# A delta-net and gated feed-forward kernel: order of all work from a list scheduler, and two units inverted in one pass

## The chip, the cores and the metric

One core of one Trainium2 chip. The metric is the device time of one execution in microseconds (us), as the median of the runs of a job. The span is the part of an execution that the profile covers; it is some 2 us shorter than the time. The granted clock is the share of full speed that TensorE was allowed, as the profile records it (PEclk). The core's engines are TensorE (PE in the profile, PEld its weight loads), VectorE (DVE), ScalarE (ACT), GpSimd (POOL) and SyncE (SP, which here only issues transfers).

## The reference

Two blocks follow each other. The first is a delta rule over 768 steps, for 4 batches of 8 heads of width 48:

```python
k_n = k / (np.linalg.norm(k, axis=-1, keepdims=True) + 1e-06)
for t in range(S):
    y[:, :, t] = np.einsum('bhd,bhde->bhe', q[:, :, t], state)
    v_old = np.einsum('bhde,bhd->bhe', state, kt)
    state = state + bt[:, :, :, None] * np.einsum('bhd,bhe->bhde', kt, vt - v_old)
```

The second takes y as 3072 tokens of 384 features through two layers, 384 to 2048 to 384, all in fp32 (the weights arrive in fp64):

```python
h = x @ w_in
g = h * np.cos(h)
return g @ w_out
```

## The kernel before

The 768 steps are cut into 24 units of 32 steps. A unit needs: transposes of k and q (`turn`, p_t), Gram products (`gram`, p_g), the inverse z of a unit lower triangular 32x32 matrix for each head and batch (`invert`), a product with the state (p_kq), a solve with z (p_u), an update of the state (p_s), an inner product (p_kq again), and transposes into the feature layout (p_z, copied into x_ffn). Two units make a pair of 256 tokens, and a pair needs 8 groups of products of the first layer (p_h) and 8 of the second (p_o).

The matrix to invert goes out to DRAM (g_dr), comes back with one head of one batch on each partition (gb), is inverted by elimination there, and goes out and back once more (z_dr, zt):

```python
def invert(n, tag=None):                 # before: one unit, 4 partitions for a matrix (SPLIT = 4)
    ...
    for j in range(C - 1):               # C = 32
        rows = j // SPLIT + 1
        shape = [128, rows, C - 1 - j]
        ...
        eng.tensor_tensor(out=part, in0=z[:, 0:rows, j, None].to_broadcast(shape),
                          in1=a[:, j, None, j + 1 :].to_broadcast(shape), op=ALU.mult)
        behind = z[:, 0:rows, j + 1 :]
        eng.tensor_tensor(out=behind, in0=behind, in1=part, op=ALU.subtract)
```

`eng` is GpSimd, for units 0 and 2 DVE. Weights come as pairs of 32-bit words and are narrowed to fp32 by two ACT steps, two DVE steps and one GpSimd addition for each of 28 tiles.

Which piece of work comes when is written out by hand, some 130 lines of calls for the head and a loop for the rest; at the end every instruction is tied to the one before it on its engine, so no engine may take another order:

```python
    inverting = {0: invert(0, "one"), 1: invert(1), 2: invert(2, "o")}
    invert_next(0, 1)
    invert_next(1, 6)
    narrow_load(2)
    ...
    for s in range(4, NU + 4):
        load(s + 8, "k")
        ...
        through_state(s)
        invert_next(s + 1, 2)
        gated(1)
        ...
```

## Time and profile before

| | before |
| --- | --- |
| time, median of 3 runs | 780.71 us (780.11 to 782.49) |
| span of the profiled run | 777.6 us |
| PE busy | 682.3 us, 88% of the span |
| DVE, ACT, POOL busy | 46%, 37%, 64% |
| bytes moved by DMA | 55.41 MB |

The share of 88% is an average over two very different stretches: it is 100% from about 200 us on, and far less before.

### The profile page before, as it was taken

How to read it: one execution, taken by the hardware profiler on the slowest of the kernel's cores; microseconds unless marked ns; L12 is line 12 of the kernel's file. 1: busy time of each engine (PE TensorE's matmuls, PEld its weight loads, DVE VectorE, ACT ScalarE, POOL GpSimd, SP SyncE). 2: the span in 40 equal slices, each digit the busy share in tenths (PEclk: the TensorE clock that was granted, in tenths of full speed). 3: DMA queues.
4: the chain of work that ended last, by engine and by line, in shares of the span. 5: the costliest groups of instructions: out<-in, count | busy, mean ns of one | idle time of the engine just before them, and what ended most of it. 6: DMA issues, size and time to landing. Idle time of an engine off the chain costs nothing.

```text
span 777.6 us, 24710 instructions
## 1 busy us (share of the span) xinstructions
PE 682.3 (88%) x10472; PEld 504.7 (65%) x10472; DVE 360.1 (46%) x694; ACT 286.8 (37%) x506; POOL 499.7 (64%) x1423
## 2 busy tenths in 40 slices
PE   4134786655999999999999999999999999999996
PEld 3133564433777777777777777777777777777763
DVE  4675765445345444444444444454444444433430
ACT  3021643344244334334434334443443333333330
POOL 6753877838877868768868678688668667710000
PEclk9995887778899999999999999999999999999999
DMA  7844567362223422332342233123222210010000
GB/s 128 221 105 111 118 133 196 82 178 69 55 49 78 88 46 58 82 62 49 72 91 44 56 83 65 45 66 77 47 47 57 61 24 10 19 25 11 10 12 20
DMA packets 164559, 55.41 MB, mean 71 GB/s; under 512 B 154512, under 2 KB 157584, under 8 KB 164448
## 3 DMA queue, kind: packets, MB, share of 16 engines
q1 hardware_dynamic: 161872, 52.79, 31.3%
q8 instruction: 82, 1.34, 0.7%
q0 software_dynamic: 448, 0.71, 0.4%
q10 hardware_dynamic: 2128, 0.33, 0.2%
q14 instruction: 29, 0.24, 0.1%
HBM read 42.78 MB, written 11.01 MB: 69 GB/s over the span
## 4 chain that ended last, share of the span: by engine, by line
PE 75%; POOL 8%; DMA 2%; issue 2%; SPq 1%; ACT 1%; DVE 0%; POOLq 0%; ACTq 0%
PE p_o L580 33%; PE p_h L552 29%; PE p_kq L447 3%; POOL z L407 3%; POOL part L400 2%; PE p_kq L504 2%; PE p_u L470 2%; PE p_t L324 2%; PE p_s L492 2%; PE p_g L340 2%; POOL w_in L225 1%; POOL w_out L225 1%; DMA gb<-g_dr 1%; PE p_z L525 1%; POOL knrm L273 1%
## 5 line engine op out<-in xcount | busy, mean ns | idle before, releaser
L552 PE MATMUL p_h<-x_ffn,w_in 128*128 128x256 f32 x1152 | 277.4, 391 | 23.4 <-POOL w_in L225 10.5
L580 PE MATMUL p_o<-w_out,g_ffn 128*128 128x384 f32 x768 | 273.4, 499 | 15.7 <-POOL w_out L225 15.0
L552 PEld LDWEIGHTS p_h<-x_ffn,w_in 128*128 128x128 f32 x1152 | 224.9, 197 | 78.4 <-POOL w_in L225 13.1
L400 POOL TENSOR_TENSOR part<-z,gb 128x60 f32<-128x60 f32 (+24 forms) x682 | 213.1, 312 | 90.4 <-ACT z L391 29.1
L407 POOL TENSOR_TENSOR z<-z,part 128x60 f32<-128x60 f32 (+24 forms) x682 | 212.1, 311 | 53.4
L580 PEld LDWEIGHTS p_o<-w_out,g_ffn 128*128 128x128 f32 x768 | 139.7, 191 | 101.8 <-POOL w_out L225 20.2
L564 DVE SCALAR_TENSOR_TENSOR r<-turns,p_h 128x512 f32<-128x512 int32 x96 | 65.9, 687 | 267.5 <-ACT turns L562 267.5
L562 ACT ACTIVATE turns<-p_h 128x512 int32<-128x512 f32 x96 | 57.2, 596 | 264.9 <-PE p_h L552 264.9
L544 DVE TENSOR_TENSOR g_ffn<-r,p_h 128x512 f32<-128x512 f32 x96 | 66.0, 687 | 66.0 <-ACT r L539 58.8
L538 ACT ACTIVATE r<-r 128x512 f32<-128x512 f32 x96 | 60.6, 631 | 72.3 <-DVE r L567 72.3
L539 ACT ACTIVATE r<-r,halfpi 128x512 f32<-128x512 f32 x96 | 69.3, 722 | 3.1
L567 DVE SCALAR_TENSOR_TENSOR r<-turns,r 128x512 f32<-128x512 int32 x96 | 68.2, 710 | 3.3
L273 POOL TENSOR_TENSOR knrm<-ksum,halves 128x16 f32<-128x16 f32 (+1 forms) x14 | 35.9, 2567 | 11.5 <-DVE ksum L270 10.5
L447 PEld LDWEIGHTS p_kq<-st,kq_t 48*32 48x32 f32 x2944 | 29.5, 106 | 7.6 <-issue 7.5
L326 ACT COPY kq_t<-p_t 128x512 f32<-128x512 f32 x48 | 25.8, 591 | 23.0 <-PE p_t L324 23.0
L447 PE MATMUL p_kq<-st,kq_t 48*32 48x48 f32 x2944 | 32.7, 213 | 0.0
L219 DVE SCALAR_TENSOR_TENSOR pairs<-pairs 128x384 uint32<-128x384 uint32 (+1 forms) x28 | 19.2, 686 | 24.4 <-ACT pairs L218 23.5
L470 PE MATMUL p_u<-rhs,zt 32*32 32x48 f32 x1472 | 23.0, 211 | 8.0 <-DMA zt<-z_dr 5.8
L340 PE MATMUL p_g<-kq_t 48*32 48x64 f32 x1536 | 22.4, 245 | 6.4 <-ACT kq_t L326 4.7
L513 ACT COPY y<-p_kq 128x384 f32<-128x384 f32 x24 | 11.5, 478 | 44.4 <-PE p_kq L504 44.4
L340 PEld LDWEIGHTS p_g<-kq_t 48*32 48x32 f32 x1536 | 18.2, 116 | 14.5 <-issue 6.3
L324 PE MATMUL p_t<-consts,qp 128*128 128x128 f32 x96 | 17.7, 316 | 10.8 <-DMA qp<-in_q_dram 10.8
(56 smaller groups left out, 449.2 us busy)
## 6 DMA issues: line engine op xcount, KB each, us to landing
gb<-g_dr SPq DMA_DIRECT2D x96, 128.0 KB
pairs<-in_moe_w_in_dram SPq DMA_DIRECT2D x12, 512.0 KB
pairs<-in_moe_w_out_dram SPq DMA_DIRECT2D x16, 384.0 KB
vp<-in_v_dram SPq DMA_DIRECT2D x96, 48.0 KB
out_dram<-o SPq DMA_DIRECT2D x24, 192.0 KB
qp<-in_q_dram SPq DMA_DIRECT2D x92, 48.0 KB
kp<-in_k_dram SPq DMA_DIRECT2D x88, 48.0 KB
z_dr<-z SPq DMA_DIRECT2D x24, 128.0 KB
```

Of the source, the lines that this page charges most:

```text
L340: nc.tensor.matmul(p_g[quarter(b), par, j], kq_t[rows48(par), 0, j, quarter(b)], kq_t[rows48(par), :, j, quarter(b)],)
L400: eng.tensor_tensor(out=part, in0=z[:, 0:rows, j, None].to_broadcast(shape), in1=a[:, j, None, j + 1 :].to_broadcast(shape), op=ALU.mult,)
L407: eng.tensor_tensor(out=behind, in0=behind, in1=part, op=ALU.subtract)
L447: nc.tensor.matmul(p_kq[quarter(b), par, a, j], kq_t[rows48(par), a, j, quarter(b)], st[rows48(par), b // 2, j, b % 2], start=(j == 0 and ...
L538: nc.scalar.activation(r, r, AF.Abs)
L539: nc.scalar.activation(r, r, AF.Sin, bias=halfpi, scale=-1.0 / SCALE)
L544: nc.vector.tensor_tensor(out=gates[p][f // 4][:, f % 4 : f % 4 + 2], in0=r, in1=p_h, op=ALU.mult)
L552: nc.tensor.matmul(p_h[:, i], w_in[:, t, (f + i) * 128 : (f + i + 1) * 128], x[:, t], start=(t == 0), stop=(t == KT - 1),)
L562: nc.scalar.activation(turns, p_h, AF.Copy, scale=1.0 / (2.0 * math.pi * SCALE))
L564: nc.vector.scalar_tensor_tensor(out=r, in0=turns, scalar=-PI2_HI * SCALE, in1=p_h, op0=ALU.mult, op1=ALU.add)
L567: nc.vector.scalar_tensor_tensor(out=r, in0=turns, scalar=-PI2_LO * SCALE, in1=r, op0=ALU.mult, op1=ALU.add)
L580: nc.tensor.matmul(p_o, gs[f // 4][:, f % 4, i * 128 : (i + 1) * 128], w_out[:, f], start=(f == 0), stop=(f == FT - 1),)
```

## The change

Its intent is to replace the hand-written order by one that a program finds when the kernel is built. Each piece of work becomes a task with an engine, a cost in us, the tasks it depends on, the buffers it takes and frees, and a time by which it is due. A list scheduler then walks through time, and each engine that is free takes the ready task that is due first. The instructions are written in that order and tied to it as before. The second part inverts the two units of a pair in one pass: 64 matrices on 128 partitions, two partitions for each, in place of four.

```diff
-SPLIT = 4
+SPLIT = 2
...
+class Order:
+    WINDOW = 132.4
+    LAG = {"PE": 0.2, "DVE": 0.15, "ACT": 0.15, "POOL": 0.2, "SP": 2.0}
+    IN_FLIGHT = 8
...
+    def run(self, wrote):
...
+            for engine, heap in ready.items():
+                if free[engine] > now:
+                    continue
+                put_back, item = [], None
+                while heap and heap[0][0] <= limit:      # earliest due first
+                    item = heapq.heappop(heap)
...
+                    if fits(item[2]):                    # are its buffers free?
+                        break
...
+                emit()                                   # the instructions are written now
...
+                free[engine] = start + cost
...
-    def invert(n, tag=None):
+    def invert(m, tag, columns):                         # m: a pair of units
...
+    VECTOR = {0: "one"}                                  # only the first pair on DVE
+    W_IN, W_OUT, LOADS = 0.3, 101.9, -30.5               # due times of the weights
+    START = 55.7
+    FIRST, STEP = 5, 5.73
...
+        ends = [0, 4, 8, 12, 16, 20, 24, C - 1]
+        for i, (x, y) in enumerate(zip(ends, ends[1:])):
+            each = (0.2, 0.001) if held else (0.245, 0.00175)     # DVE, GpSimd: us per instruction, per element
+            cost = sum(2 * (each[0] + each[1] * (j // SPLIT + 1) * (C - 1 - j)) for j in range(x, y))
+            add(("inv", m, i), "DVE" if held else "POOL", cost, ...)
...
+            add(("hidden", *key), "PE", 2.62, lambda f=f: hidden(p, f), deps, ...)
+            add(("gate", *key), "DVE", 0.73, lambda f=f: hidden_gate(p, f), ...)
...
-    norms(0, one)
-    load(3, "k", nc.gpsimd)
-    load(2, "k")
-    turn(0)
-    ...                                                  # 200 lines of order by hand
+    log = order.run(wrote)
```

## The prediction

> **What bounds the kernel now.** I read the 40 slices of the page first, then the busy times by stretch, then the chain that ended last, then the waits of the first 200 us.
>
> The slices (19.4 us each; the digits are tenths of busy time):
>
> ```profile
> PE   4134786655999999999999999999999999999996
> POOL 6753877838877868768868678688668667710000
> PEclk9995887778899999999999999999999999999999
> DMA  7844567362223422332342233123222210010000
> ```
>
> There are two regimes. From slice 11 (about 200 us) to the end TensorE is busy at full clock. Before that it is neither busy nor at full clock, and no other engine is full either. The stretches give the sizes (length, then busy us of each engine, granted clock, DMA share):
>
> ```profile
> core 0: us, PE busy (x) PEld busy (x) DVE busy (x) ACT busy (x) POOL busy (x), PEclk, DMA share, GB/s
> 0.00:76.76 76.76, 28.14 (x751) 22.52 (x751) 48.42 (x183) 16.19 (x33) 45.30 (x111) 0.88 0.64 139
> 76.76:200.94 124.18, 84.30 (x1337) 60.61 (x1337) 64.63 (x118) 55.58 (x104) 90.26 (x190) 0.78 0.52 125
> 200.94:771.40 570.46, 569.83 (x8386) 421.54 (x8385) 247.07 (x393) 214.51 (x370) 364.15 (x1123) 1.00 0.25 51
> 255.05:309.20 54.15, 54.15 (x896) 40.59 (x901) 24.94 (x41) 21.31 (x37) 41.30 (x126) 1.00 0.32 66
> ```
>
> The cuts are mine: 76.76 is the start of the first p_h product, 771.40 the last p_o product, and 255.05 to 309.20 one pair of units in the steady part. A pair costs TensorE 54.15 us at full clock. The chain of waits shows 2.59 us for a p_h group and 2.58 us for four p_o blocks; a pair has 8 of each, 41.3 us, so two units of delta-net work take 12.85 us. Twelve pairs are 649.8 us; unit 0 has no product with the state (1.42) and unit 23 no update (about 0.8): **TensorE owes about 648 us at full clock**. Since 570 of these lie after 200.94, only 78 us' worth was done in the first 201 us. **The loss is 201 - 78 = 123 us**, and after 771.4 come 6.2 us of last copy and store. That loss is the only thing of size to win.
>
> The loss is not one bound but hand-over after hand-over. The waits of the first 200 us:
>
> ```profile
> ACT w_out L216 <- DMA pairs<-in_moe_w_out_dram: 26.9, 4, 11.6
> DVE pairs L219 <- ACT pairs L218: 23.5, 9, 10.9
> PE p_u L470 <- DMA zt<-z_dr: 19.8, 8, 13.1
> POOL w_out L225 <- DVE w_out L224: 16.4, 3, 8.0
> PE p_o L580 <- POOL w_out L225: 15.0, 4, 7.0
> PE p_t L324 <- DMA qp<-in_q_dram: 10.8, 1, 10.8
> PE p_h L552 <- POOL w_in L225: 10.5, 5, 6.4
> ```
>
> ACT stands before a weight load that has not landed, DVE behind ACT, GpSimd behind DVE, TensorE behind GpSimd. And the chain that ended last shows why the weight was late:
>
> ```profile
> 145.24 2.26 DMA z_dr<-z
> 154.12 4.54 DMA gb<-g_dr
> 162.41 3.27 DMA pairs<-in_moe_w_out_dram
> 178.20 3.90 POOL w_out L225 x4
> 193.57 4.21 PE p_o L580 x6
> ```
>
> In between (not shown) lie the SyncE issues of zt, of the q, k, v loads and of gb: the weight load was queued behind a put that waited for an inversion. The order written by hand costs the time, not the amount of work.
>
> **What the Trainium skill says.** "TensorE: Matmul & The Clock Gate", section "Architectural detail: the array is 16× 32×32, not 1× 128×128", says that ACT, DVE and GpSimd run their instructions strictly in order. The trace agrees: the 26.9 us above are a whole engine held by one load. The same page, Part 1, says that the clock falls to half after an idle window and comes back after some 3.4 us of work. It agrees: from 60 to 80 us the granted clock is 0.50, and the first p_h group takes 5.46 us instead of 2.59. So filling gaps pays twice. "GPSIMD Engine Reference", section 3.1, says that an element costs GpSimd more than DVE and that dispatch is a large fixed part; here the 60-element product takes 0.30 us on GpSimd (undisturbed) and 0.22 on DVE. "DMA: Bandwidth & Descriptors", section Specifications, puts line rate at 512 B or more; of 164559 packets 154512 are under 512 B, and the first 40 us have a DMA share of 0.81 at only 176 GB/s. DMA is the scarce thing there.
>
> **The change, part by part.**
>
> *Inversion.* Per unit: 31 steps of two instructions, 62 in all, 1560 elements per partition for each of the two kinds (sum of rows times columns left). Per pair with two rows' shares: still 62 instructions, 2856 elements for each kind. GpSimd goes from 0.21 us (8 elements) to 0.325 (76), so about 0.195 + 0.0017 per element, plus 0.075 between instructions. Unit now: 62 x 0.27 + 3120 x 0.0017 = 22.0 us (the trace: 23.0 to 45.9). Pair after: 62 x 0.27 + 5712 x 0.0017 = 26.4 us instead of 44. GpSimd falls from 41 to about 25 busy us per 54; as TensorE is full there, this by itself is worth nothing after 200 us. In the head it frees GpSimd for the 28 weight additions (32 us). On DVE (0.163 + 0.001 per element, 0.04 between): the first pair takes 62 x 0.203 + 5.7 = 18.3 us; before, units 0 and 2 were done there.
>
> *Traffic.* gb was fetched four times per unit, 96 x 128 KB = 12.6 MB. Now it is twice per pair, 24 x 256 KB = 6.3 MB. In the first 40 us that is 1 MB of some 7.
>
> *First p_h.* Before: unit 0 was solved at 51.1 us, but unit 1 only at 66.0, because its z was put and fetched through the SyncE queue separately; p_h began at 76.76. After: both come out of one inversion. g of unit 1 is ready at 15.5; put and fetch about 6 us with no queue ahead, more with the weight loads, which the due times put first: inversion starts at 22 to 26. With 18.3 us and about 3 us of other DVE work it ends at 44 to 47. From its end to the end of the first solve were 8.6 us (42.5 to 51.1). Then, from the trace's durations: u 1.0, p_s 1.5, st 1.0, p_kq 1.4, rhs 0.55, second solve 1.5, u 1.0, p_s and the inner product 3.0, y 0.5, p_z 0.6, x 0.5: 12.6 us. **First p_h at 65 to 68, say 66.**
>
> *After that.* Done by then: units 0 and 1 and the transposes and Gram products of some four more, about 18 us' worth, leaving 630. Weights are loaded as early as buffers allow, so the first and second layer of pair 0 and units 2 and 3 all offer work, and I allow 8 us for cold clock and gaps from 66 to about 120 (before: of the 78 us' worth some 16 were done by 76.76, so 62 fell into the 124 us up to 200.94, a loss of 62 us).
>
> *Steady part and tail.* The due-time rule reaches for the next ready task. Its costs (2.62 for a p_h group, 0.9, 0.85, 1.4 for the small ones) sum to 54.2 us per pair, which is what the trace shows, and its DVE and ACT costs are slightly above the trace's. I expect no large waits. The tail stays: 6 us.
>
> **Sum:** 66 + 630 + 8 + 6 = 710 us of span, and the time is some 2 to 3 us above the span (780.7 against 777.6): **712 us**.
>
> **The rivals.**
> 1. *Fine waits on TensorE.* Before, at least one p_o and one p_h group (5.2 us) lay between two small products of a unit, which hid DVE and ACT. The list may place them the moment its model calls them ready. If 6 hand-overs of each of 24 units cost 0.3 us, that is 43 us, and the time is about 755. For: orders are pinned, so an error of the model is a wait. Against: a 2.6 us block usually lies between, and the costs match.
> 2. *DMA holds the head.* Ten weight loads at the front are 5 MB, at 176 GB/s almost 30 us; the put and fetch of g queue behind them, the first p_h comes at 78 or so, with the weights ready. Then 78 + 630 + 6 + 6 + 2.5: about 723. For: share 0.81 already. Against: half of gb is gone, and large loads run above the mean rate.
> 3. *Shared buffers.* Weight pairs and gates share ten buffers; weights of the second layer waiting for narrowing could hold the gates, or ACT and DVE (28 x 1.3 and 28 x 1.1 us of narrowing) become the bound from 60 to 130. About 735. Against: between 76.76 and 200.94 DVE is 52% and ACT 45% busy.
> 4. *Only the inversion counts*, order is neutral: first p_h 10 us earlier, the rest as before, about 768. Against: the waits above are order.
>
> **Range and chances.** Rivals 2 and 3 in part are likely and set the upper end; the lower end is a first p_h at 60 with no loss after it. 698 to 733. Over 2% faster means under 765; only rival 4 or two rivals in full miss it: 0.94. Within 2%: 0.04; slower: 0.02.
>
> **What would show it.** Right: p_h first at about 66; TensorE near 90% busy from about 70 and full clock from 90; the steady pair still 54 us; GpSimd's inversion groups half the count, and about 430 busy us down to about 240; gb 24 issues; ACT's wait for w_out gone. Wrong: TensorE waits spread over the steady part (rival 1), zt waits beyond 70 us (rival 2), gates waiting for GpSimd (rival 3), or a second half where pairs take over 55 us.

## More of the kernel before

The cosine of the first layer is done like this, for each p_h group:

```python
nc.scalar.activation(turns, p_h, AF.Copy, scale=1.0 / (2.0 * math.pi * SCALE))   # ACT, to int32
nc.vector.scalar_tensor_tensor(out=r, in0=turns, scalar=-PI2_HI * SCALE, in1=p_h, ...)  # DVE, 1st reduction step
nc.vector.scalar_tensor_tensor(out=r, in0=turns, scalar=-PI2_LO * SCALE, in1=r, ...)    # DVE, 2nd reduction step
nc.scalar.activation(r, r, AF.Abs)
nc.scalar.activation(r, r, AF.Sin, bias=halfpi, scale=-1.0 / SCALE)
nc.vector.tensor_tensor(out=gates..., in0=r, in1=p_h, op=ALU.mult)               # DVE, the gate: frees p_h's bank
```

p_h lies in PSUM, in a buffer that the text calls a bank. The kernel has two of them, so the p_h group after the next can't start before the gate has freed one.

## The result and the profile after

Faster, by less than half of what I had predicted. Ratios in this document are the mean time of one kernel's fast runs over that of the other's fast runs of the same rounds, so they are not quite the ratios of the medians beside them.

| | before | after | predicted |
| --- | --- | --- | --- |
| time, median of 4 runs each | 781.04 us | 754.67 us (754.30 to 759.42) | 712 (698 to 733) |
| ratio | | 0.9675 (95% interval 0.9633 to 0.9716) | 0.91 |
| span of the profiled run | 777.6 us | 752.7 us | 710 |
| first p_h product | 76.8 us | 79.2 us | 66 |
| a pair of units in the steady part | 54.15 us | 54.2 to 57.9 us | 54 |
| POOL busy | 499.7 us | 345.6 us | |
| bytes moved by DMA | 55.41 MB | 49.18 MB | 49.1 |

The slices of the changed kernel (18.8 us each, tenths of busy time):

```profile
PE   3206899798999999999999999999999999999996
POOL 6379648938606706706806805804705606500000
PEclk9755899999999999999999999999999999999999
DMA  9895481455222132232132132122021111100000
```

Against the slices of before, PE is near full from the fifth slice on instead of from the eleventh: that is the gain. But the first three slices together hold less than before (3, 2 and 0 against 4, 1 and 3), the third and fourth are at a granted clock of 0.5, and DMA is at 0.8 to 0.9 in the first three. And the slices of the steady part hide something, since a 9 is anything from 90%. The stretches show it (length; PE, PEld, DVE, ACT, POOL busy with instruction counts; granted clock, DMA share, GB/s), cut at the first p_h product:

```profile
0.00:79.23 79.23, 27.92 (x879) 23.48 (x879) 53.25 (x142) 29.13 (x52) 53.51 (x88) 0.67 0.76 165
79.23:200.00 120.77, 107.64 (x1640) 80.45 (x1636) 70.39 (x121) 56.79 (x102) 82.79 (x150) 0.96 0.51 111
200.00:500.00 300.00, 290.67 (x4676) 215.31 (x4675) 135.65 (x228) 115.20 (x193) 137.91 (x316) 0.98 0.27 53
500.00:750.00 250.00, 245.85 (x3287) 177.47 (x3285) 95.96 (x142) 88.10 (x147) 71.35 (x186) 1.00 0.13 27
```

From 200 to 500 us TensorE now stands still for 9.3 us. Before it stood still for 0.6 us of 570 there. The list of waits over the whole span names what is new (total us, times, longest):

```profile
POOL part L528 <- DMA gb<-g_dr: 228.2, 11, 27.2
...
DVE knrm L413 <- POOL knrm L402: 41.8, 9, 9.6
```

The first line costs nothing: GpSimd is early with its work and waits for the next pair's matrices, some 21 us per pair. The second is a wait of DVE for the norms of k that GpSimd makes after an inversion, up to 9.6 us long. Before, this wait came to 2.3 us in all. Four of the nine lie before 200 us (at 12, 84, 155 and 199 us), five in the steady part. What it does is seen around 315 us. TensorE's timeline (start, length, instruction; in brackets the idle time before it and what ended it):

```profile
314.17 2.75 PE L671 MATMUL p_h<-x_ffn,w_in 128*128 128x256 f32 x12
316.85 0.86 PE L461 MATMUL p_g<-kq_t 48*32 48x64 f32 x64
319.51 4.35 PE L671 MATMUL p_h<-x_ffn,w_in 128*128 128x256 f32 x12 [1.80 <-DVE g_ffn L707]
```

DVE's and GpSimd's of the same moment:

```profile
313.14 0.69 DVE L693 SCALAR_TENSOR_TENSOR r<-turns,r 128x512 f32<-128x512 int32 x1
317.75 0.17 DVE L413 TENSOR_SCALAR knrm<-knrm 128x16 f32<-128x16 f32 x1 [3.92 <-POOL knrm L402]
...
318.77 0.68 DVE L707 TENSOR_TENSOR g_ffn<-r,p_h 128x512 f32<-128x512 f32 x1
```

```profile
314.64 0.23 POOL L535 TENSOR_TENSOR z<-z,part 128x16 f32<-128x16 f32 x1
314.82 2.90 POOL L402 TENSOR_TENSOR knrm<-ksum,halves 128x16 f32<-128x16 f32 x1
```

GpSimd finishes an inversion at 314.9 us and only then takes the norms, to 317.7. DVE's order has the scaling that needs these norms before a gate, so it stands still for 3.92 us with the gate behind it. The gate would have freed a p_h bank, so TensorE stands still for 1.80 us, and the group after that is slow as well, 4.35 us in place of 2.75, because the clock has fallen. The same happens once per pair: gaps of 1.80, 1.80, 1.52, 1.80 and 1.80 us before p_h groups at 263, 320, 377, 433 and 491 us, and in three of the five the group behind is at the slower clock.

### The profile page after: what moved, and what is told of

The parts are those of the page before. It is cut to its first block, busy times and chain, and to the rows that moved or that the text cites. A ratio compares the mean times of both kernels' runs of the same rounds, so it can differ in the third digit from the quotient of the medians.

```text
span 752.7 us, 23817 instructions
## 1 busy us (share of the span) xinstructions
PE 672.1 (89%) x10472; PEld 496.7 (66%) x10472; DVE 355.2 (47%) x632; ACT 289.2 (38%) x493; POOL 345.6 (46%) x738
## 2 busy tenths in 40 slices
DMA packets 162695, 49.18 MB, mean 65 GB/s; under 512 B 154208, under 2 KB 157296, under 8 KB 162592
## 3 DMA queue, kind: packets, MB, share of 16 engines
q8 instruction: 82, 1.34, 0.8%
## 4 chain that ended last, share of the span: by engine, by line
PE 40%; POOL 31%; DMA 13%; issue 6%; SPq 5%; DVE 3%; ACT 1%; ACTq 0%; POOLq 0%; DVEq 0%
PE p_h L671 17%; PE p_o L718 16%; POOL z L535 14%; POOL part L528 13%; DMA gb<-g_dr 5%; SPq L283 3%; DMA kp<-in_k_dram 3%; DMA g_dr<-g 2%; PE p_kq L570 2%; POOL knrm L402 2%; DMA z_dr<-z 1%; POOL w_in L375 1%; PE p_t L443 1%; POOL w_out L375 1%; SPq L553 1%
## 5 line engine op out<-in xcount | busy, mean ns | idle before, releaser
L671 PE MATMUL p_h<-x_ffn,w_in 128*128 128x256 f32 x1152 | 271.1, 388 | 13.3 <-DVE g_ffn L707 13.3
L718 PE MATMUL p_o<-w_out,g_ffn 128*128 128x384 f32 x768 | 269.7, 496 | 2.8 <-POOL w_out L375 2.2
L671 PEld LDWEIGHTS p_h<-x_ffn,w_in 128*128 128x128 f32 x1152 | 219.6, 194 | 54.0 <-DVE g_ffn L707 9.5
L528 POOL TENSOR_TENSOR part<-z,gb 128x126 f32<-128x126 f32 (+22 forms) x341 | 132.7, 389 | 253.6 <-DMA gb<-g_dr 228.2
L535 POOL TENSOR_TENSOR z<-z,part 128x126 f32<-128x126 f32 (+22 forms) x341 | 138.7, 407 | 26.7
L443 PE MATMUL p_t<-consts,kp 128*128 128x128 f32 x96 | 17.3, 309 | 47.6 <-DMA pairs<-in_moe_w_in_dram 32.3
L443 PEld LDWEIGHTS p_t<-consts,kp 128*128 128x128 f32 x96 | 12.5, 157 | 50.2 <-issue 45.1
L605 DVE TENSOR_TENSOR u<-p_u,bz 128x768 f32<-128x768 f32 x24 | 22.9, 954 | 34.7 <-PE p_u L597 34.7
L626 DVE TENSOR_TENSOR st<-st,p_s 128x768 f32<-128x768 f32 x22 | 20.9, 952 | 33.0 <-PE p_s L618 33.0
L728 ACT ACTIVATE o<-p_o 128x384 f32<-128x384 f32 x24 | 11.8, 490 | 43.2 <-PE p_o L718 42.1
```

Source lines behind the costliest of these rows:

```text
L671: nc.tensor.matmul(p_h[:, i], w_in[:, t, (f + i) * 128 : (f + i + 1) * 128], xts[p][:, t], start=(t == 0), stop=(t == KT - 1),)
L718: nc.tensor.matmul(p_os[p, i], gates[p, k][:, f % 4, i * 128 : (i + 1) * 128], w_out[:, f], start=(f == 0), stop=(f == FT - 1),)
```

## The experiments

Fifteen kernels ran on the chip. The kernel before, run beside them, gave medians from 779.52 to 782.78 us. The prediction had 42.7 us too little span. So the questions were: what is lost in the steady part, what makes the first p_h late, and whether order or pairing brought the gain.

### The cost of GpSimd in the list

The list plans an inversion of a pair at 62 x 0.245 + 5712 x 0.00175 = 25.2 us. In the steady part of the trace it takes 29.0. One constant was changed:

```diff
-            each = (0.2, 0.001) if held else (0.245, 0.00175)
+            each = (0.2, 0.001) if held else (0.31, 0.0018)
```

> Only the two numbers change with which the list plans an inversion on GpSimd: 0.31 + 0.0018 per element instead of 0.245 + 0.00175, so 29.5 us for a pair instead of 25.2; the trace of the changed kernel shows 29.0 to 29.3. The instructions are the same, only their order moves. Theory (the list believed GpSimd 4 us per pair faster than it is, so DVE's scale stands in its queue before a gate and waits for GpSimd's norms, the p_h bank stays taken and TensorE stops): the steady pair falls from 56 to 58 us back to 54 or 54.5, DVE's wait for knrm from 41.8 us to under 10, and the time to 728 to 740. Rival (small products placed too tightly on TensorE, or cold clock and DMA in the head alone): the pair stays at 56 to 58 and the time at 750 or above.

Measured: 736.12 us (734.65 to 738.76), ratio 0.9449. The stretches of this kernel, cut at its first p_h product:

```profile
80.26:200.00 119.74, 111.14 (x1738) 84.07 (x1727) 78.04 (x139) 61.16 (x109) 81.86 (x147) 0.99 0.50 106
200.00:500.00 300.00, 300.00 (x4909) 221.78 (x4910) 139.05 (x226) 119.98 (x200) 139.43 (x333) 1.00 0.28 54
```

TensorE is busy for all of the 300 us, pairs take 54.6 us, and the wait for the norms has come down from 41.8 us to 3.0:

```profile
DVE knrm L413 <- POOL knrm L402: 3.0, 2, 1.8
```

The inversion hardly got faster (28.4 to 29.0 us in the steady part); the list only no longer plans work behind it that comes too early. This is 18.6 us in the medians. About half of it comes before the steady part: the first p_h of the third pair is at 186.0 us in place of 195.2.

A second way to the same end left the wrong cost and held the scaling back behind a gate:

```diff
-                [("norms", m, a), ("beta",)])
+                [("norms", m, a), ("beta",)] + ([("gate", m - 4, 4)] if m >= 4 else []))
```

> The wrong cost stays; one dependence is added, so that from pair 4 on the scale of norms is placed on DVE behind the gates of the first three p_h groups. Theory (the wait for knrm in front of a gate stops TensorE): the gap of 1.5 to 1.8 us per pair before a p_h group goes, the pair falls to 54 to 55 from about 300 us on, and the time to 738 to 745; less than by the right cost, as everything behind GpSimd is still planned 4 us early and the second hundred us don't change. Rival (the wait is harmless, the pair is long for another reason): 750 to 755.

Measured: 746.12 us (744.67 to 749.73), ratio 0.9573, just above the range expected. Pairs take 54.3 us except one of 55.2 and one of 59.0, where the order slips again. So in the steady part the chain of norms, scaling, gate and bank is the path. Repairing it by hand from pair 4 on gives half of what the right cost gives, as nothing changes before that: the third pair's first p_h stays at 194.7 us.

### Order alone

The list as it is, but each unit inverted alone again, with four partitions for a matrix, units 0 and 2 on DVE, and a fitting cost:

```diff
-SPLIT = 2
+SPLIT = 4
-    VECTOR = {0: "one"}
+    VECTOR = {0: "one", 2: "o"}
-            each = (0.2, 0.001) if held else (0.245, 0.00175)
+            each = (0.2, 0.001) if held else (0.29, 0.0018)
```

> The list schedules, but each unit is inverted by itself as before (rows on four partitions, gb fetched four times per unit, units 0 and 2 on DVE), with an inversion on GpSimd planned at 0.29 + 0.0018 per element, 23.6 us, which is what the kernel before shows. If the order alone makes the gain and pairing only relieves GpSimd and DMA, which are not the bound: 735 to 755. If pairing is what shortens the head (both units of the first pair out of one inversion): first p_h back at 80 to 85 and the time 755 to 775.

Measured: 772.11 us (769.17 to 774.27), ratio 0.9897. A pair in its steady part:

```profile
276.10:333.80 57.70, 56.25 (x834) 42.52 (x834) 26.40 (x39) 23.70 (x41) 46.51 (x156) 1.00 0.28 53
```

The list alone gives 1%. The two parts of it are far larger and cancel. The first p_h of the third pair comes at 197.7 us, 34 us earlier than the 232.0 of the kernel before, although the very first p_h is late (81.6 us). The nine pairs from there to the last one's first p_h take 520.1 us in place of 479.0. So most of the head was won without the pairing (with the pairing and a fitting cost the third pair starts at 186.0 us). What the order wins is given back at 57.7 us per pair against 54.15. GpSimd is busy for 46.5 us of a pair, but DVE's wait for its norms, 1.4 us in all from 200 to 500 us, is not the reason. TensorE stands still once per pair for 1.6 to 2.1 us about half way through the 64 small products of a Gram product, and some groups behind are at half clock:

```profile
354.82 0.49 PE L461 MATMUL p_g<-kq_t 48*32 48x64 f32 x28
357.02 0.48 PE L461 MATMUL p_g<-kq_t 48*32 48x64 f32 x33 [1.71 <-issue]
```

The list of waits names nothing for it ("issue"), but the trace shows what it goes with. The DMA queue q8 brings 82 packets of 16 KB, 1.34 MB in all; TensorE runs 21100 instructions, so by size a packet is 256 of them, at some 64 bytes each. Counted from the start, each of the six pauses between 355 and 645 us ends at the same place in such a block (instruction 193 of 256), 1.3 to 1.5 us after the end of a q8 packet. Over all runs, 47 of the 48 pauses of this kind (over 0.4 us, put down to "issue", between two products of the same sort) end at that place, 1.2 to 1.9 us after a packet; the kernel before has none. So it looks as if TensorE had used up its instructions before the next block was there. In this list the Gram product follows the 128 products of the state at once, and up to the pause the two are some 320 instructions in 1.7 us. In the hand-written order a p_o and a p_h group lie between them (5.4 us). No run was made that puts them back, so this is read from the traces and not tested.

So this run shows that the list without the pairing gains little, and the traces point to small products set too close together as at least a part of the reason. It does not show that GpSimd's slack is the reason.

### Why GpSimd's inversion is dear

My own working had 26.4 us for an inversion, and 29.0 came. I took from the changed kernel's trace every instruction of the 11 inversions on GpSimd, and set each against the lower quartile of its own line and shape, as the duration without disturbance. Together they are 25.4 us over, 2.3 us per inversion, and the excess depends on what DVE ran at the same time (smaller groups left out):

| DVE instruction that overlapped most | its inputs | overlaps | excess us |
| --- | --- | --- | --- |
| second reduction step, r from turns and r | two in SBUF | 40 | 12.8 |
| weighing, vp from vp and knrm | two in SBUF | 19 | 7.1 |
| first narrowing step, pairs from pairs | two in SBUF | 17 | 3.4 |
| first reduction step, r from turns and p_h | one in SBUF, one in PSUM | 65 | 0.06 |
| gate, g_ffn from r and p_h | one in SBUF, one in PSUM | 49 | 0.08 |
| second narrowing step, w_out shifted in place | one in SBUF | 8 | 1.0 |
| none | | 372 | 0.4 |

Two inputs in SBUF are not the only way: DVE's second narrowing step has one and is in the way too, in few overlaps.

One such pair of instructions, in GpSimd's timeline and in DVE's:

```profile
309.46 0.36 POOL L535 TENSOR_TENSOR z<-z,part 128x91 f32<-128x91 f32 x1
309.90 0.67 POOL L528 TENSOR_TENSOR part<-z,gb 128x78 f32<-128x78 f32 x1
310.65 0.35 POOL L535 TENSOR_TENSOR z<-z,part 128x78 f32<-128x78 f32 x1
```

```profile
309.68 0.69 DVE L693 SCALAR_TENSOR_TENSOR r<-turns,r 128x512 f32<-128x512 int32 x1
```

The 78-element product of 309.90 takes 0.67 us, its neighbours of 91 and 78 elements 0.36 and 0.35. It began inside DVE's second reduction step and ended 0.20 us after it. To test it, one operand of that step was read from PSUM instead, in the changed kernel with its wrong cost. The result is slightly wrong:

```diff
-            out=r, in0=n, scalar=-PI2_LO * SCALE, in1=r, op0=ALU.mult, op1=ALU.add
+            out=r, in0=p_hs[p, f], scalar=-PI2_LO / 6.0, in1=r, op0=ALU.mult, op1=ALU.add
```

> The changed kernel with its wrong cost of GpSimd and with one operand of DVE's second reduction step exchanged: it reads p_h from PSUM in place of the turns in SBUF, same instruction, same shape, same place. The result is slightly wrong on purpose. If DVE's instructions with two SBUF inputs hold up GpSimd: the inversions of the steady part fall from 29.0 us to 27.7 to 28.1, nothing is left of the 0.3 us that an overlap with this step cost, DVE waits less for GpSimd's norms, and the time falls from 754.7 to 742 to 752 us. If they don't: 28.8 to 29.3 us each, and 753 to 757.

Measured: 741.02 us (738.57 to 744.32), ratio 0.9483, a little below the range. The inversions of the steady part take 27.8 us. The step still takes DVE 0.69 us, but 56 overlaps with it now cost GpSimd 0.08 us in all. TensorE's gaps before p_h groups shrink from 1.5 to 1.8 us to between 0.4 and 1.1, and none lets the clock fall. So in this order 13.7 us of time hung on which memory one operand of another engine lay in.

Does that instruction cost anything once the list knows GpSimd's true cost? In the next two kernels the reduction takes a single step, with 2 pi in fp32. One is built on the kernel with the right cost, the other on the first set of tuned constants below:

```diff
-            out=r, in0=n, scalar=-PI2_HI * SCALE, in1=p_hs[p, f], op0=ALU.mult, op1=ALU.add
-        )
-        nc.vector.scalar_tensor_tensor(
-            out=r, in0=n, scalar=-PI2_LO * SCALE, in1=r, op0=ALU.mult, op1=ALU.add
+            out=r, in0=n, scalar=-2.0 * math.pi * SCALE, in1=p_hs[p, f], op0=ALU.mult, op1=ALU.add
-            add(("rest", *key), "DVE", 1.45, lambda f=f: hidden_rest(p, f),
+            add(("rest", *key), "DVE", 0.72, lambda f=f: hidden_rest(p, f),
```

> e1 with the argument of the cosine reduced in one step of DVE (turns times 2 pi in fp32) in place of two, and the cost of that task in the list halved: DVE does 96 x 0.7 us = 67 us less, and none of it with two SBUF inputs. e1 has TensorE 300.00 busy of 300 us in the steady part, so there nothing is to be won. If e1's rest lies in the head and in TensorE's own work: 730 to 737 us (e1: 736). If DVE still held up TensorE between 80 and 200 us, where e1 leaves it idle for 8.6 us: 724 to 730.

> The same in e9_tuned_a, whose other constants made no difference to e1: 728 to 736 by the first theory, 720 to 728 by the second.

Measured: 737.66 us (735.89 to 742.79, ratio 0.945) and 736.12 us (734.41 to 738.82, ratio 0.9412). DVE's busy time falls from 354.9 to 286.9 and 290.4 us, the inversions to 27.8 and 27.2 us, and the time does not move. The same instruction was worth 13.7 us where the list did not know GpSimd's time and nothing where it did.

### The head

First, should the weights step aside for the first inversion? Their DVE steps were held back from the fourth tile on:

```diff
-        add(("shift", t), "DVE", 1.25 * c, lambda: narrow_shift(t), [("split", t)])
+        add(("shift", t), "DVE", 1.25 * c, lambda: narrow_shift(t), [("split", t)] + ([("inv", 0, 6)] if t >= 3 else []))
```

> On top of the corrected cost of e1 (736 us): DVE's narrowing of the weights from the fourth tile on waits until the inversion of the first pair is done. Theory (the head is a trade: the first p_h was late because DVE narrowed weights between the steps of the first inversion, which took 23.3 us instead of 18, but those weights are needed right after): the inversion ends 5 us earlier, first p_h at 74 to 77, but the weights come later and the second hundred us lose it again, so 734 to 744. Rival (the first p_h sets the end, as the prediction reckoned): 728 to 732.

Measured: 749.70 us (749.12 to 751.48), ratio 0.9584: slower than without, and above the ranges of both theories. The inversion ended at 47.9 us, 4 us earlier, but the first solve then waited for DVE's weighing of v and began at 61.2, and the first p_h came at 88.8.

Or should their loads stand behind the first fetch of g?

```diff
-            [("weights", t - 1)] if t else [],
+            ([("weights", t - 1)] if t else []) + ([("gram_get", 0)] if t >= 1 else []),
```

> On top of e1: all weight loads but the first are issued only after the fetch of g of the first pair, so that put and fetch of g find the queue free. If the weight loads in front hold the chain (rival 2 of the prediction): the inversion starts at 24 to 26 instead of 29, first p_h at 74 to 77, time 728 to 734. If DMA is simply short in the first 60 us, so that what is not loaded early is missing later: first p_h no earlier than 78, the weights late, time 738 to 748.

Measured: 748.17 us (746.74 to 750.32), ratio 0.9569. The first solve began 5 us earlier, at 55.5, but then the next product waited 8.21 us for DVE, and the first p_h came at 80.4, as in the kernel with the right cost alone. The weights were later (the last was narrowed at 154.0 us in place of 146.8) and the second pair paid for it: its first p_h came at 138.9 in place of 126.3. The time is just above the range of the second theory.

Is it the cold clock? Thirteen fillers of two small products each were put on TensorE among the products of units 0 and 1:

```diff
+    for i in range(13):
+        add(("fill", i), "PE", 0.45, lambda i=i: fill(i),
+            [AFTER[i]] + ([("fill", i - 1)] if i else []),
+            makes=[] if i else [("h", ("p_w",))], uses=[("p_w",)], due=95)
```

> On top of e1: 13 fillers of two products of the identity with itself (into a p_h bank, never read) are put on TensorE between the small products of units 0 and 1, to keep the clock up; the order of all else is the same. If the cold clock lengthens the chain from the first solve to the first p_h (17.3 us; 12.6 by warm durations in the prediction): the granted clock in 60 to 80 us rises from 0.5 to 0.8 or more, first p_h comes 3 to 4 us earlier, at 76 to 77, and the time is 732 to 734. If the clock is a symptom only: first p_h and time as in e1 or 1 to 2 us later.

Measured: 736.54 us (735.11 to 737.22), ratio 0.9416, against 736.12 without. The granted clock from 60 to 80 us rose from 0.56 to 0.83, and the first p_h came at 81.8 instead of 80.3. So keeping the clock up in this way gains nothing. What a warm clock alone would be worth is not shown, since the fillers themselves took 7.3 us of TensorE between the first solve and the first p_h. But the expectation has one thing wrong: the 12.6 us of my prediction were not warm durations. Its 1.5 us for p_s and for the inner product are those of the kernel before at half clock (1.56 and 1.50; 0.89 and 0.88 here with the fillers). So the cold clock was in that sum already.

Then three kernels took work out of the head instead of moving it: all weight work held back until unit 1 is in x; weights loaded but hardly narrowed; weights narrowed but not loaded (a constant tile is read). The last two give wrong results.

```diff
-            [("weights", t - 1)] if t else [],
+            [("weights", t - 1)] if t else [("features_out", 1)],
```

> e1 with all weight loads held back until unit 1 is copied into x, so that the chain g, inversion, z, solves, y, x of units 0 and 1 runs with no weight traffic on DMA and no narrowing on ACT and DVE beside it. In e1 that copy of unit 1 into x ended at 79.3 us and the first p_h began at 80.3. Theory 1, the 13 us by which the first p_h was later than I predicted are other work standing in the chain's way: the copy ends at 64 to 69 us. Theory 2, the chain itself is longer than I summed it (small products at half clock, puts and fetches slower than taken): it ends at 72 to 78 us. The time of the whole is of no interest: the weights come late, I expect 760 to 780.

```diff
-        nc.scalar.activation(lo, lo, AF.Copy, scale=2.0**-29)
...
-        nc.vector.scalar_tensor_tensor(out=lo, in0=hi, ...)
-        nc.vector.tensor_scalar(w, w, 3, None, op0=ALU.logical_shift_left)
...
-        nc.gpsimd.tensor_tensor(out=w, in0=w, in1=words.pop(t)[:, :, 0], op=ALU.add)
+        words.pop(t)
```

> e1 with the weights still loaded, but narrowing cut to a single ACT instruction per tile: no second conversion on ACT, no two DVE steps, no addition on GpSimd. The result is wrong on purpose; only the times matter. Theory 1a, what delays the chain and the stretch from 80 to 190 us is the narrowing on ACT, DVE and GpSimd: first p_h at 66 to 72 (e1: 80.3), third pair's first p_h at about 170 to 178 (e1: 186.0), span about 710 to 720. Theory 1b, it is the weight traffic on DMA and the issue of the loads on SyncE: first p_h at 76 to 80, third pair at 182 or later, span 725 to 733.

```diff
-        nc.sync.dma_start(out=words[t], in_=src)
...
-        nc.scalar.activation(dst, hi.bitcast(FP), AF.Copy, scale=2.0**-111)
-        nc.scalar.activation(lo, lo, AF.Copy, scale=2.0**-29)
+        nc.scalar.activation(dst, hold[:, 0:n], AF.Copy, scale=2.0**-111)
+        nc.scalar.activation(words[t][:, :, 0], hold[:, 0:n].bitcast(U32), AF.Copy, scale=2.0**-29)
```

> The other half of e8: e1 with every narrowing instruction of the weights on ACT, DVE and GpSimd in its place and order, but no weight loaded at all (the conversions read a constant tile instead). The result is wrong on purpose. Known so far: the first solve ended at 62.2 us in e1, at 52.3 with neither loads nor narrowing beside it (e7), at 59.6 with loads and without most of the narrowing (e8). If the loads on the DMA queues are what delays the chain: the first solve ends at 52 to 56 us, the first p_h begins at 69 to 74, the span is 715 to 726. If loads and narrowing delay it each on its own, and removing either leaves the other: the first solve ends at 58 to 62, the first p_h begins at 76 to 80, the span is 726 to 733.

Measured, in us from the start of the span, with what my prediction had:

| kernel | inversion on DVE | z put | first solve ends | unit 1 in x | first p_h | span |
| --- | --- | --- | --- | --- | --- | --- |
| predicted | 22-26 to 44-47 | | 53.4 | | 66 | 710 |
| after | 28.9 to 52.2 | 52.9 | 62.0 | | 79.2 | 752.7 |
| right cost | 29.0 to 51.8 | 52.5 | 62.2 | 79.3 | 80.3 | 732.9 |
| no weight work (chain alone) | 25.4 to 43.5 | 44.2 | 52.3 | 70.6 | (78.1) | 771.2 |
| loads, hardly any narrowing | 28.7 to 46.8 | 47.5 | 59.6 | 74.9 | 78.3 | 732.4 |
| narrowing, no loads | 26.9 to 47.6 | 48.3 | 57.6 | 73.4 | 73.9 | 727.9 |

(53.4 is the predicted 66 less the 12.6 that I had from the first solve to p_h. In the chain alone the p_h product waited for its weights.) These three had one run each.

Three things follow. With no weight work beside it, the chain up to the first solve takes what I had worked out, 52.3 us against 53.4. The 9.9 us that the right-cost kernel is later than that are not one cost: without loads it is 4.6 us earlier, without narrowing 2.6, without both 9.9. The expectations don't separate their theories cleanly. In the first, 70.6 lies between the ranges. In the second, all three figures lie in the ranges for the loads (first p_h 78.3, third pair 185.4, span 732.4), while the inversion, 18.1 us in place of 22.8, shows the narrowing. In the third, the end of the solve (57.6) lies between the ranges, the p_h in the first and the span in the second. Last, all this is worth little for the whole: taking every load of weights away gains 5 us of span, taking most narrowing away half a microsecond.

After the first solve, no kernel came near 12.6 us. In the kernel without loads it is 16.3, from 57.64 to 73.95. TensorE's timeline there:

```profile
60.30 1.50 PE L635 MATMUL p_kq<-u,tt 32*32 32x48 f32 x64
62.40 0.55 PE L652 MATMUL p_z<-consts,y 128*128 128x128 f32 x3 [0.60 <-ACT y L646]
...
72.64 1.37 PE L570 MATMUL p_kq<-st,kq_t 48*32 48x48 f32 x128
73.95 5.45 PE L671 MATMUL p_h<-x_ffn,w_in 128*128 128x256 f32 x24
```

The inner product of unit 0 at 60.30, the wait for its copy, its transposes at 62.40 and the state product of unit 2 at 72.64 all stand on TensorE before the first p_h. I had summed the path of unit 1 alone.

The last attempt at the head freed the DMA queues of what is not used before 80 us, the k and q loads from unit 5 and the v loads from unit 2, on top of the right cost:

```diff
+            if n == (2 if x == "v" else 5):
+                deps.append(("put", 0))
```

> e1 with the k and q loads from unit 5 on and the v loads from unit 2 on held back until z of the first pair is put. In e1 these stand in SyncE's queue between 32 and 51 us, in packets of 192 B, and none is used before 80 us. If the DMA queues of the head are the limit and these loads are the part that can wait: the first solve ends 3 us or more earlier than e1's 62.2 and the time is 724 to 732. If what is taken out of the head comes back later, as in e4 and e5 (v and k, q arriving late for units 2 to 5): 735 to 745.

Measured: 740.56 us (740.50 to 742.20), ratio 0.9481. The first solve ended at 63.8, later than without. In this order 7.2 us of the narrowing lay on DVE between the steps of the first inversion, where it was 4.2 us with the right cost alone, and the inversion ended at 54.6 us in place of 51.8: the list had filled the gap with other work.

### Other constants

Two sets of the list's constants, with the same instructions. Of the first set, without its five transfer times:

```diff
-    WINDOW = 132.4
+    WINDOW = 105.7
-    W_IN, W_OUT, LOADS = 0.3, 101.9, -30.5
-    START = 55.7
-    FIRST, STEP = 5, 5.73
+    W_IN, W_OUT, LOADS = 36.7, 99.4, -5.8
+    START = 33.9
+    FIRST, STEP = 5.84, 4.91
...
-            each = (0.2, 0.001) if held else (0.245, 0.00175)
+            each = (0.2, 0.001) if held else (0.358, 0.0018)
```

> The list with other constants and the same instructions: GpSimd's cost 0.358 us per instruction, window 105.7, due times of the weights 36 us later, k, q, v transfers at 2.06 us instead of 1.6, pairs closer together in their due times. If what is left beside the cost of GpSimd is a matter of where the list puts the weights against the first pair: 716 to 728 us, with the third pair's first p_h before 178. If the head is bound by its work whatever the order: 730 to 740, no better than e1's 736.

> The same with a second set of constants: GpSimd's cost 0.327, the w_out weights due 37 us earlier, w_in loads 15 us earlier, transfers of g and z dearer. Same two theories as for e9_tuned_a: 716 to 728 if the constants decide, 730 to 740 if not.

Measured: 735.81 us (732.17 to 737.35, ratio 0.9418) and 740.34 us (737.65 to 741.89, ratio 0.9479). The first is inside the range of the second theory, the other just above it. Their first p_h came at 84.7 and 81.0 us. Neither beats the single right constant. Four kernels of quite different heads lie between 735.8 and 736.6 us (right cost, fillers, first tuned set, that set with one reduction step), all 18 us faster than the changed kernel, and none of what I tried goes below them.

## Why the prediction was wrong

The direction was right and the size was not: 712 predicted, with 733 as the upper end, and 754.67 measured. By its own steps:

**The loss before the change, and that order makes it: right as to the head.** The 123 us lost before 200 us were there to be won. Of them the changed kernel won 24.9 us of span and the kernel with the right cost 44.7. The list with single inversions won 34 us up to the third pair, so my fourth rival, that order is neutral, doesn't hold there. But it lost 41 us after that, and order alone wins 1%. The pairing alone I did not run.

**"Steady part: I expect no large waits": wrong, and the largest miss.** I had checked the list's costs against the trace for TensorE, ACT and DVE, and found them to fit. I did not check GpSimd's, although I had written down 26.4 us of my own beside the list's formula. The list has 25.2, the chip takes 29.0, and the difference comes out through two engines as a gap on TensorE once per pair. My first rival said that an error of the model is a wait, since orders are pinned, and that the time would then be about 755. I set it aside with "the costs match". It is what happened, with one wait of 1.5 to 1.8 us per pair and in three of five a half-clock group behind it, in place of many small ones. That the time is also the rival's 755 is luck: it had 43 us of small waits, where the wrong cost makes 20.8 and the rest of the miss lies elsewhere. The loss did not stay in the steady part: about 9 us of what the wrong cost lost came before the first p_h of the third pair.

**"Pair after: 26.4 us": wrong by 2.6.** Where DVE has no second reduction step, the inversions of the steady part take 27.2 us (the tuned kernel with one step), so 0.8 of the 2.6 are in my fixed and per-element parts and 1.8 are disturbance. (The 2.3 us per inversion above are a mean with the first two, which have the narrowing beside them.) What I left out is that DVE's instructions hold up GpSimd's. The Trainium skill, "GPSIMD Engine Reference", section "Specifications", gives the SBUF interfaces as shared with VectorE, with contention against DVE instructions in a 2-port mode or with two SBUF inputs. I had read section 3.1 of the same page for the cost per element and stopped there. The trace agrees: 12.8 us over in 40 overlaps with a step of two SBUF inputs, 0.06 in 65 with one of a single SBUF input, and the experiment that exchanged the operand took it away.

**"By itself worth nothing after 200 us": not confirmed.** Without the pairing the same list takes 57.7 us for a pair and 17 us more in all. (The right-cost kernel is 36 us faster than it, and there both lists have a fitting cost.) What shows in its steady part is TensorE's pause inside the Gram product, and by the q8 packets that looks like a matter of the order. So the runs neither bear the sentence out nor show it wrong. GpSimd's inversion groups came down to 271 us (132.7 + 138.7) and not to 240, in part for the reason just given.

**"First p_h at 66": wrong by 13.2.** Of these, 8.6 are before the end of the first solve (62.0 against 53.4). They come from the weights: their loads on DMA and their narrowing on DVE and ACT, each with a part, as my second rival had it for DMA ("the first p_h comes at 78 or so"). I had allowed 3 us for other work on DVE. The other 4.6 (17.3 us from the solve to p_h against 12.6) are a mis-sized term of the sum, mostly unit 0's inner product and transposes and unit 2's state product on TensorE. Some 0.9 are unit 1's own: its solve took 2.0 us where I had 1.5, and its state product 1.8 where I had 1.4. The inversion itself was right, 18.1 us without disturbance against 18.3.

**"After that: 8 us, 630 left": nearly right without the steady waits.** After the first p_h the changed kernel has TensorE busy for 107.6 + 290.7 + 245.9 = 644.2 us and not busy for 23.0 up to its last product at 746.4, together 29.2 more than 638. With the right cost it is 637.2 and 9.2, together 8.4 more. So 20.8 us of the miss are GpSimd's cost in the list; 8.4 stay. Of the 8.4, 7.2 are busy time: a steady pair takes 54.6 us with TensorE never idle where it took 54.15 before, which is some 4 us over eleven pairs, one pair near the end takes 56.3, and less had been done before the first p_h than I assumed. Why a full pair takes 0.4 us longer I did not look into.

**Two looser readings.** The 26.9 us of ACT before w_out are four waits, the longest of 11.6 us, and not one load. And they don't test whether an engine keeps its order by itself, since in these kernels the program ties each instruction to the one before it.

**Tail of 6 us and 24 fetches of gb: right**, with 6.3 us and 24. ACT's wait for w_out, which I expected to be gone, shrank to 9.4 us from 26.9 between 80 and 200 us.

The sum: 20.8 (a wrong cost in the list) + 8.6 (weights in the way of the first solve) + 4.6 (terms left out between solve and p_h) + 8.4 (TensorE's time after it) = 42.4, and 0.3 of the tail.

What stays open: no order that I tried turns a shorter head into time. Which loads and narrowing would have to come when, so that neither the first nor the second pair waits, I have not found. Each dependency that I added moved the rest of the list as well, so the four attempts do not show that it can't be done.

## What to carry to other kernels

A scheduler with pinned orders is as good as its worst cost, and a cost that is 13% too low on an engine that is half idle can cost 18 us through a short task queued behind it. So check every engine's costs against the trace, the idle ones first. A cost that is too high seems to do less harm: with 0.358 us per instruction, 32.5 us for an inversion of 29, and other constants, the time was the same 735.81 us. Don't let the list set long runs of small products side by side: by the traces, though not by a test, TensorE runs out of instructions there. And look at which operands lie in SBUF when DVE and GpSimd work at the same time. Before optimising what a trace shows as slow, ask whether the time still hangs on it, as the same instruction was worth 13.7 us in one order and nothing in another.

## What the Trainium skill lacked or had wrong

- "GPSIMD Engine Reference", "Specifications", names the contention in one row and gives no size there; the skill says more of these interfaces in "SBUF — State Buffer", on which this document does not draw. The size here is 0.32 us for a GpSimd instruction that overlaps most with a 0.69 us DVE instruction with two SBUF inputs (12.8 us in 40 overlaps), and 0.001 us with one whose other input is in PSUM (0.06 in 65). An in-place shift with one SBUF input cost 1.0 us in 8 overlaps.
- "TensorE: Matmul & The Clock Gate", Part 1, gives an idle window of some 3.4 us after which the clock falls. In the changed kernel gaps of 1.80 us were enough in three cases (4.35, 4.54 and 4.54 us for the next p_h group) and not in another of the same length (2.86 us). The page does tell of a kernel whose clock swings with short gaps; what length is enough it does not say.
- "Runtime: NRT & Kernel Launch", "Instruction fetch mechanics", names no case in which a straight run of small products outruns the fetch of TensorE's instructions. Here pauses of 0.5 to 3.3 us inside such runs, which the profile puts down to "issue", end at the same place of a block of 256 instructions in 47 of 48 cases, 1.2 to 1.9 us after a 16 KB packet of queue q8.
